# Raw weights of the first expert block in one tile per product, their differences and the gate's steps in another order

## The chip, the core and the metric

The kernel runs on one core of a Trainium2 chip. It is measured in device microseconds (us) from the first to the last instruction. Five engines have queues of their own: TensorE (PE, matrix products), VectorE (DVE), ScalarE (ACT), GpSimd (POOL) and SyncE (SP, which here only issues DMAs). Each runs its list in order and waits on semaphores of the others.

## What is computed

Attention with two masks, then a small mixture of three weight matrices, then a second mixture of eight experts whose gate is normalised by rows and columns eight times. The change lies in the last part:

```python
def _moe2_ref(x, w_gate, w1, w2):          # x: 2304 x 512, w1: 8 x 512 x 1024, w2: 8 x 1024 x 512
    logits = x @ w_gate
    P = np.exp(logits - logits.max())
    for _ in range(8):
        P /= P.sum(1, keepdims=True) + 1e-09
        P /= P.sum(0, keepdims=True) + 1e-09
        P *= N / E
    out = np.zeros((N, D), dtype=np.float32)
    for e in range(E):
        h = np.maximum(x @ w1[e], 0.0)
        out += P[:, e:e + 1] * (h @ w2[e])
    return out
```

## The kernel before

Products keep 32-bit accuracy: every operand is split into a high part (a rounding copy on ACT, L68) and the rest (a subtraction, L69, on POOL for weights), and each product is three passes over such parts (high x high, high x rest, rest x high).

Tokens go in three blocks of 768. The change is in the first of them, where the weights of the experts are prepared as well and kept in DRAM for the two other blocks. This block has 32 stages (L788), one for each of 8 experts `e` and 4 pairs `n` of 128 hidden columns. A stage computes a quarter of x @ w1[e] by a scheme of Strassen's kind, in 7 products of 6 matmuls each (`product`, L803) instead of 8. It needs the weights as they are (`A1` for A11 and A12, `A2` for A22) and differences of them (`S12`, `S34`), made by `sums_w2` (tile `sums`, L538) on DVE and split by `split_w2` (tile `wa`). The products accumulate in two PSUM banks, `p` and `q`, which swap roles from stage to stage, and DVE and ACT turn them into `h`: DVE adds a kept copy (`plus`, L859, tiles `m` and `u`), ACT applies the relu (L853), DVE takes the rest (L854). Between the products PE runs the second product of the stage before (`second`, which calls `Before.tile`, L757), six pieces of 6 matmuls. In the first stage of an expert the finished sums of the expert before are added to the output by an `acc` operation of DVE behind each of the six pieces (L776).

The order of PE in a stage is A11, A12, piece, S2, piece, S1, piece, S3, piece, S4, piece, A22, piece. A12 overwrites the bank that A22 of the stage before filled, so it waits for the two reads of `halves(1, 0, p)`.

Other work runs beside that:

- The raw weights of a stage come in two `raw` tiles, each with rows of w1 and of w2 side by side (`fetch_w2`). The pool has four such tiles.
- The second product's weights are split into `wb` (`split_out`), and their differences are made for the later blocks: `sums_out` (tile `ts`, L577, four operations on DVE) and `keep_out` (split into `tw`, and stored from there).
- In stages 1 to 5 the gate's normalisation runs in steps (`sinkhorn`), some eight small DVE operations at a time (L722 to L739, with L735 reading PSUM), with a small matmul on PE (L734) between, in the bank that `free[0]` names.
- In stages 16, 17, 30 and 31 differences of x for a later block are made (`sums_x`, L602, tiles `xd` and `xh`).

PE, ACT and DVE keep the order in which the code is written. POOL and SP are put in order by a scheduler, with the due times that it reckons. A stage of the code before asks for the next stage's `sums` behind S2, for two gate steps ahead of S2, and ends with `ts` and the next loads:

```python
        second(1, 0)
        more_w("A1")
        window()                       # two steps of the gate
        product(p, "S2", "T2", False, False)
        nc.scalar.copy(u2, p)
        if nxt:
            s_next[0] = sums_w2(nxt)
```

Of the kernel before, what the change touches and what calls it, by code (L numbers as in the profile page):

```python
# [9 lines left out]
F32 = mybir.dt.float32  # L10
# [34 lines left out]
E, F2 = 8, 1024  # L45
P = 128
# [15 lines left out]
NPAIR = NF2 // 2  # L62
# [23 lines left out]
def attention_moe(ctx: ExitStack, tc: tile.TileContext, q, k, v, mask, wm1, wg, wm2, out):  # L86
    nc = tc.nc
# [13 lines left out]
    raw_p = ctx.enter_context(tc.tile_pool(name="raw", bufs=4))  # L101
# [371 lines left out]
    qk, vs, raws = {}, {}, {}  # L473
# [48 lines left out]
    stages = [(0, e, n) for e in range(E) for n in range(NPAIR)]  # L522
    UP = ("A1", "S12", "S34", "A2")

    def fetch_w2(e, n):
        raws = [raw_p.tile([P, 2, 512], F32, name="raw") for _ in range(2)]
        for i in range(2):
            nc.sync.dma_start(raws[i], wm2[e, 2 * n + i])
        return raws

    def sums_w2(raws):
        s = sm_p.tile([P, 4, 256], F32, name="sums")
        (a11, a12), (a21, a22) = ((r[:, 0, 0:256], r[:, 0, 256:512]) for r in raws)
# [10 lines left out]
        for i, name in enumerate(HOLD[what]):  # L544
            ops[name] = t[:, :, i * 256:(i + 1) * 256].rearrange("p s (k m) -> p s k m", k=2)

    def split_w2(i, what, raws, s):

        src = {
            "S12": lambda: s[:, 0:2].rearrange("p o n -> p (o n)"),  # L550
            "S34": lambda: s[:, 2:4].rearrange("p o n -> p (o n)"),
            "A1": lambda: raws[0][:, 0],
            "A2": lambda: raws[1][:, 0, 256:512],
        }[what]()
# [9 lines left out]
        nc.sync.dma_start(t[:, :, 0:w].bitcast(F32), wsd[i % len(stages), UP.index(what), :, :, 0:w])  # L564
        named(w_ops.setdefault(i, {}), what, t)

    def split_out(raws, i):
        t = wb2_p.tile([P, 2, 512], F32R, name="wb2")
        split(nc, t[:, 0], t[:, 1], raws[i][:, 1], nc.gpsimd)
        return t  # L570

    def sums_out(raws):

        s = wt_p.tile([P, 4, 256], F32, name="ts", bufs=1)
        (b11, b12), (b21, b22) = ((r[:, 1, 0:256], r[:, 1, 256:512]) for r in raws)
# [46 lines left out]
    def early():  # L622

        for i in range(2):
            ahead_w[i] = fetch_w2(0, i)
        *_, src = sums_x(fetch_x(0, nc.scalar))
        for i in range(2):
            s = sums_w2(ahead_w[i])
            for what in ("A1", "S12", "S34", "A2"):
                split_w2(i, what, ahead_w[i], s)  # L630
# [5 lines left out]
    ahead_w = {}  # L636

    ahead, starts, gates_due, unit = {}, [], {}, 0
    for what in WORK:
# [147 lines left out]

    for i, (blk, e, n) in enumerate(stages):  # L788
        wo, xo = w_ops.pop(i), x_ops[blk]
        raws = ahead_w.pop(i)  # L790
        nxt = ahead_w.get(i + 1) if i else None
        if i + 2 < len(stages):
            ahead_w[i + 2] = None
        near, last = (e == E - 1 and n == NPAIR - k for k in (2, 1))
        far, farther = (e == E // 2 and n == k for k in (0, 1))
        if near or far:
# [16 lines left out]
                k = NSUB * j + t  # L813
                nc.scalar.mul(acc[k], acc[k], prob[:, k, 0:1])

        def window():
            if i:
                next(gate, None)
                next(gate, None)

        def more_w(what):
            if nxt:
                split_w2(i + 1, what, nxt, s_next[0])
            if i == len(stages) - 1:
# [46 lines left out]
        plus(q, m1)  # L871
        halves(0, 0, m1)
        if i:
            keep_out(i - 1, ts)
        more_x("B21")
        sum_x(last or farther)
        second(1, 0)
        more_w("A1")
        window()
        product(p, "S2", "T2", False, False)  # L880
        nc.scalar.copy(u2, p)
        if nxt:
# [19 lines left out]
        halves(1, 1, m5)  # L902
        sum_x(near or far)
        second(0, 0)
        ws = [split_out(raws, 0)]
        if i == 0:
            gates_turn(B - 1)
            ps_a.release()
# [3 lines left out]
        plus(q, u2)  # L912
        halves(0, 1, u2)
        more_x("B22")
        sum_x(near or far)
        second(0, 1)
        more_w("A2")
        next(gate, None)
        product(p, "A22", "T4", False, True)
        halves(1, 0, p)  # L920
        if i:
            next(gate, None)
        ws.append(split_out(raws, 1))
# [12 lines left out]
    for j in (1, 0):
# [16 lines left out]
    def fetch_out(e, n):  # L953
        t = raw_p.tile([P, 2, 512], F32, name="raw")
        for f in range(2):
            nc.sync.dma_start(t[:, f], wm2[e, 2 * n + f, :, 1])
        return t
# [80 lines left out]

    acc.clear()
    NS = len(stages)  # L1040
    outs = {0: [fetch_out(0, n) for n in range(NPAIR)]}
    for g in range((NBLK - 1) * E):
        blk, e = 1 + g // E, g % E
        sec = Second(blk, e, outs.pop(g))
# [79 lines left out]
        for u in range(len(units)):  # L1124
            sec.product(u)
            if u % NPAIR == NPAIR - 1:
                sec.ready(u // NPAIR)
            if u < 2:
                sec.rows(2 * NPAIR - 2 + u)
                sec.mix(2 + u)  # L1130
            if 2 * NPAIR <= u + 6 < len(units):
                sec.rows(u + 6)
            if 3 * NPAIR <= u + 10 < len(units):
                sec.weight(u + 10)
            if u == 18 and g + 1 < (NBLK - 1) * E:
# [72 lines left out]
```

## Time and profile before

| what | us |
|---|---|
| median of 3 runs | 1917.85 |
| lowest and highest run | 1915.32, 1920.61 |
| span of the profiled execution | 1916.7 |
| PE busy in it | 1864.0 (97%) |
| DVE busy | 1234.4 (64%) |
| ACT busy | 969.2 (51%) |
| POOL busy | 712.5 (37%) |

The profile is of one execution, whose time is its span. The first expert block lies between 428 and 940 us; what stands ahead of it is attention and the first mixture, what follows are the two other blocks. Busy shares are means over parts with different limits, so the block has to be read by itself: which waits PE has in it, and who ends them. A row of the timeline gives the start and the duration of an operation (or of a run of equal ones, with their number), and in brackets how long the engine sat idle before it and who ended that.

### The profile page before, as it was taken

The page shows a single profiled execution, that of the slowest core. Times are in us where ns is not written, and L with a number is a line of the kernel's source. Part 1 is how long each engine was busy: PE and PEld are TensorE (multiplying, and loading weights), DVE is VectorE, ACT ScalarE, POOL GpSimd, SP SyncE. Part 2 cuts the span into 40 slices and gives each one's busy share as a digit, 9 for nine tenths or more (in the row PEclk, how much of TensorE's full clock was granted, in tenths as well). Part 3 has the DMA queues.
Part 4 walks back from the last instruction along what each step waited for, and adds up shares of the span by engine and source line. Part 5 has one row for each costly group of instructions (what it writes and reads, how often), then busy time and mean ns, then how long its engine had stood idle before and what let it go on. Part 6 is the DMA issues. An engine that isn't in the chain of part 4 may idle for free.

```text
span 1916.7 us, 35287 instructions
## 1 busy us (share of the span) xinstructions
PE 1864.0 (97%) x12873; PEld 1793.7 (94%) x12873; DVE 1234.4 (64%) x2227; ACT 969.2 (51%) x2337; POOL 712.5 (37%) x603
## 2 busy tenths in 40 slices
PE   6889999999999999999999999999999999999999
PEld 5789999998899988899899999999999999999999
DVE  7984333426766676666676667766676666766667
ACT  5663544324454444444455555555546555565554
POOL 5663433435566667666611112111112121121211
PEclk8999999999999999999999999999999999999999
DMA  8644444446666669666986767767798767777673
GB/s 266 229 172 160 156 149 160 142 154 217 230 250 250 248 247 330 254 253 248 342 291 216 231 219 221 257 215 226 228 346 254 227 217 224 221 254 227 214 226 111
DMA packets 206542, 435.32 MB, mean 227 GB/s; under 512 B 18848, under 2 KB 97312, under 8 KB 204832
## 3 DMA queue, kind: packets, MB, share of 16 engines
q1 hardware_dynamic: 203680, 429.12, 66.3%
q10 hardware_dynamic: 2688, 3.93, 0.7%
q8 instruction: 102, 1.67, 0.3%
q14 instruction: 72, 0.59, 0.1%
HBM read 313.97 MB, written 119.01 MB: 226 GB/s over the span
## 4 chain that ended last, share of the span: by engine, by line
PE 83%; DVE 7%; DMA 5%; ACT 2%; issue 2%; POOL 1%; SPq 0%; ACTq 0%; DVEq 0%; POOLq 0%
PE po L1006 24%; PE po L1074 12%; PE po L757 10%; PE ps L380 10%; PE q L1074 6%; PE p L1074 6%; PE p L803 5%; PE q L803 5%; PE ps L400 3%; DMA cx<-in_wm 1%; DMA raw<-in_wm 1%; DVE ts L577 1%; DVE h L854 1%; DMA x2s<-xg 1%; PE pst L226 1%
## 5 line engine op out<-in xcount | busy, mean ns | idle before, releaser
L1006 PE MATMUL po<-wt,hop 128*128 128x256 f32 x4032 | 490.3, 284 | 2.1 <-DMA wt<-wtd 2.1
L1006 PEld LDWEIGHTS po<-wt,hop 128*128 128x128 f32 x4032 | 487.8, 192 | 4.1 <-ACT wt L68 2.3
L69 POOL TENSOR_TENSOR wt<-raw,wt 128x256 fp32r<-128x256 f32 x192 | 170.3, 908 | 780.0 <-ACT wt L68 767.8
L69 DVE TENSOR_TENSOR hop<-r,hop 128x384 fp32r<-128x384 f32 x384 | 224.4, 611 | 226.8 <-ACT hop L68 223.2
L757 PE MATMUL po<-wb,h 128*128 128x512 f32 x1152 | 295.6, 393 | 0.9 <-POOL wb L69 0.9
L380 PE MATMUL ps<-xt,wa 128*128 128x288 f32 x1728 | 244.0, 300 | 5.3 <-DVE h L69 3.1
L757 PEld LDWEIGHTS po<-wb,h 128*128 128x128 f32 x1152 | 214.3, 188 | 34.9 <-POOL wb L69 1.7
L380 PEld LDWEIGHTS ps<-xt,wa 128*128 128x128 f32 x1728 | 234.6, 191 | 8.4 <-DVE h L69 3.5
L68 ACT CAST hop<-r 128x384 fp32r<-128x384 f32 x384 | 188.0, 514 | 96.3 <-DVE r L991 74.0
L69 POOL TENSOR_TENSOR wa<-raw,wa 128x512 fp32r<-128x512 f32 x112 | 135.5, 1214 | 76.5 <-ACT wa L68 76.0
L1088 ACT ACTIVATE r<-r 128x384 f32<-128x384 f32 x192 | 99.9, 525 | 117.3 <-DVE r L1087 117.3
L1074 PE MATMUL po<-xT,wa 128*128 128x384 f32 x768 | 155.9, 338 | 0.0
L1074 PEld LDWEIGHTS po<-xT,wa 128*128 128x128 f32 x768 | 136.7, 188 | 0.0
L69 POOL TENSOR_TENSOR tw<-ts,tw 128x512 fp32r<-128x512 f32 x64 | 83.8, 1332 | 95.3 <-DVE h L854 70.6
L1074 PE MATMUL po<-xB,wa 128*128 128x384 f32 x576 | 116.9, 338 | 0.0
L69 POOL TENSOR_TENSOR wa<-sums,wa 128x512 fp32r<-128x512 f32 x64 | 87.3, 1384 | 57.5 <-ACT wa L68 36.8
L1074 PEld LDWEIGHTS po<-xB,wa 128*128 128x128 f32 x576 | 102.5, 188 | 0.0
L69 POOL TENSOR_TENSOR wb<-raw,wb 128x512 fp32r<-128x512 f32 x64 | 93.6, 1462 | 23.5 <-ACT wb L68 22.9
L980 DVE TENSOR_TENSOR r<-r,r 128x384 f32<-128x384 f32 x128 | 93.1, 727 | 2.2
L68 ACT CAST wa<-raw 128x512 fp32r<-128x512 f32 x112 | 61.6, 555 | 59.5 <-DMA raw<-in_wm 32.4
L538 DVE TENSOR_TENSOR sums<-raw 128x256 f32<-128x256 f32 x64 | 41.5, 650 | 74.1 <-DMA raw<-in_wm 73.9
L1019 ACT COPY mm<-po 128x256 f32<-128x256 f32 x144 | 47.0, 376 | 71.0 <-PE po L1006 71.0
(185 smaller groups left out, 3135.7 us busy)
## 6 DMA issues: line engine op xcount, KB each, us to landing
wa<-wsd SPq DMA_DIRECT2D x192, 512.0 KB, 4.4
wt<-wtd SPq DMA_DIRECT2D x256, 256.0 KB, 3.5
wsd<-wa SPq DMA_DIRECT2D x96, 512.0 KB, 3.4
raw<-in_wm SPq DMA_DIRECT2D x64, 512.0 KB, 4.3
wtd<-tw SPq DMA_DIRECT2D x128, 256.0 KB, 2.9
raw<-in_wm SPq DMA_DIRECT2D x128, 256.0 KB, 5.2
wa<-wsd SPq DMA_DIRECT2D x64, 256.0 KB, 4.5
cx<-in_wm SPq DMA_DIRECT2D x12, 1024.0 KB, 6.8
```

Of the source, the lines that this page charges most:

```text
L68: nc.scalar.copy(hi, src)
L69: sub.tensor_tensor(out=lo, in0=src, in1=hi.bitcast(F32), op=ALU.subtract)
L380: nc.tensor.matmul(ps, w[:, wi, kk], xt[:, xi, kk, n0:n0 + HB], start=(n == 0), stop=(n == 3 * KT - 1),)
L400: nc.tensor.matmul(ps, wo[f][:, wi, d2 * P:(d2 + 1) * P], hs[f][:, hi, a * HB:(a + 1) * HB], start=(f == 0 and n == 0), stop=(f == NF1 - 1 ...
L538: nc.vector.tensor_tensor(out=s[:, o], in0=x, in1=y, op=op)
L757: nc.tensor.matmul(po, self.hs[f, j][:, hi, t * P:(t + 1) * P], self.ws[f][:, wi], start=(n + f + k == 0), stop=(n == NPAIR - 1 and f == 1 ...
L803: nc.tensor.matmul(ps, wo[w][:, wi, kk], xo[x][:, xi, kk], start=(first and k == 0), stop=True if k == 5 else False, skip_group_check=not ...
L980: nc.vector.tensor_tensor(out=r[o, n], in0=r[x, n], in1=r[y, n], op=op)
L1006: nc.tensor.matmul(self.ps[side, t][:, 0:256], h[:, hi, t * P:(t + 1) * P], w[:, wi], start=(first and i == 0), stop=(n == NPAIR - 1 and i ...
L1019: nc.scalar.copy(m, ps)
L1074: nc.tensor.matmul(ps[k][side], wo[k][w][:, wi, kk], xo[x][:, xi, kk], start=(first and c == 0), stop=c == 5, skip_group_check=not first,)
L1088: nc.scalar.activation(out=r, in_=r, func=AF.Relu)
```

## The change

- A `raw` tile no longer holds rows of w1 and w2 side by side. `fetch_w2` takes a third argument and loads, by two DMAs of 256 KB, either the w1 part of both row groups (`ups`) or the w2 part (`downs`). `fetch_out` of the later blocks, which did this already, is gone in its favour.
- A stage's w1 tile is loaded behind the last use of the tile two stages ahead of it (`fetch_up(i + 3)` behind the split of `A2`), its w2 tile in the stage before (`fetch_down(i + 1)`).
- `sums_out` moves from the end of a stage into the next stage, behind `plus` and the first `halves`.
- The two gate steps that stood ahead of S2 come one behind S2 and one behind `sums`.
- The second step of `sum_x` of stages 16 and 30 moves from behind `halves(0, 1)` to behind `halves(1, 0)`.

```diff
-    def fetch_w2(e, n):
-        raws = [raw_p.tile([P, 2, 512], F32, name="raw") for _ in range(2)]
-        for i in range(2):
-            nc.sync.dma_start(raws[i], wm2[e, 2 * n + i])
-        return raws
+    def fetch_w2(e, n, part):
+        t = raw_p.tile([P, 2, 512], F32, name="raw")
+        for f in range(2):
+            nc.sync.dma_start(t[:, f], wm2[e, 2 * n + f, :, part])
+        return t
+
+    def fetch_up(i):
+        if i < len(stages):
+            ups[i] = fetch_w2(*stages[i][1:], 0)
+
+    def fetch_down(i):
+        if i < len(stages):
+            downs[i] = fetch_w2(*stages[i][1:], 1)
...
         for i in range(2):
-            ahead_w[i] = fetch_w2(0, i)
+            fetch_up(i)
+        for i in range(2):
+            fetch_down(i)
...
-        def window():
+        def step():
             if i:
                 next(gate, None)
-                next(gate, None)
...
         halves(0, 0, m1)
         if i:
-            keep_out(i - 1, ts)
+            keep_out(i - 1, sums_out(downs.pop(i - 1)))
+            fetch_down(i + 1)
         more_x("B21")
         sum_x(last or farther)
         second(1, 0)
         more_w("A1")
-        window()
         product(p, "S2", "T2", False, False)
         nc.scalar.copy(u2, p)
-        if nxt:
+        step()
+        if nxt is not None:
             s_next[0] = sums_w2(nxt)
+        step()
...
         more_x("B22")
-        sum_x(near or far)
         second(0, 1)
         more_w("A2")
+        if i:
+            fetch_up(i + 3)
         next(gate, None)
         product(p, "A22", "T4", False, True)
         halves(1, 0, p)
-        if i:
-            next(gate, None)
-        ws.append(split_out(raws, 1))
-        ts = sums_out(raws)
+        sum_x(near or far)
+        step()
+        ws.append(split_out(down_raw, 1))
         more_x("T3")
         keep_x(3)
         keep_x(4)
         second(0, 2)
         more_x("T4")
-        if i + 2 < len(stages):
-            ahead_w[i + 2] = fetch_w2(*stages[i + 2][1:])
```

The lists of ACT and POOL are the same before and after. DVE's list, from the last gate operation of stage 2 into stage 3 (`m` is `plus`, `h` the rest of a relu, `sms` a sum of the gate that reads PSUM in L735), before:

```order
L729 TENSOR_REDUCE sms<-prob 128x8
L577 TENSOR_TENSOR ts<-raw 128x256
L577 TENSOR_TENSOR ts<-raw,ts 128x256
L577 TENSOR_TENSOR ts<-raw 128x256
L577 TENSOR_TENSOR ts<-raw,ts 128x256
L859 TENSOR_TENSOR m_5519<-p,m_5519 128x384
L854 SCALAR_TENSOR_TENSOR h_5513<-m_5519,h_5513 128x384
L735 TENSOR_SCALAR sms<-p 128x8
L737 RECIPROCAL sms<-sms 128x8
L738 TENSOR_SCALAR sms<-sms 128x8
```

The same place after (the line numbers have moved by 8 to 12):

```order
L741 TENSOR_REDUCE sms<-prob 128x8
L868 TENSOR_TENSOR m_5524<-p,m_5524 128x384
L863 SCALAR_TENSOR_TENSOR h_5518<-m_5524,h_5518 128x384
L585 TENSOR_TENSOR ts<-raw 128x256
L585 TENSOR_TENSOR ts<-raw,ts 128x256
L585 TENSOR_TENSOR ts<-raw 128x256
L585 TENSOR_TENSOR ts<-raw,ts 128x256
L747 TENSOR_SCALAR sms<-p 128x8
L546 TENSOR_TENSOR sums<-raw 128x256
L546 TENSOR_TENSOR sums<-sums,raw 128x256
L546 TENSOR_TENSOR sums<-raw 128x256
L546 TENSOR_TENSOR sums<-raw,sums 128x256
```

The four `ts` have moved behind `m` and `h`, and the four `sums` of the next stage, which came behind eight operations of the gate, follow L735 at once.

PE's list in stage 3, from A11 to the piece behind S2, before:

```order
L803 MATMUL q<-xB_4297,wa 128x384 x6
L803 MATMUL p<-xB_4329,wa 128x384 x6
L757 MATMUL po_5212<-wb_5454,h_5344 128x512 x3
L757 MATMUL po_5212<-wb_5495,h_5346 128x512 x3
L734 MATMUL p<-sms,ones 128x8
L803 MATMUL q<-xT_4822,wa 128x384 x6
L757 MATMUL po_5238<-wb_5454,h_5344 128x512 x3
```

And after:

```order
L813 MATMUL q<-xB_4297,wa 128x384 x6
L813 MATMUL p<-xB_4329,wa 128x384 x6
L769 MATMUL po_5221<-wb_5465,h_5347 128x512 x3
L769 MATMUL po_5221<-wb_5509,h_5349 128x512 x3
L813 MATMUL q<-xT_4832,wa 128x384 x6
L746 MATMUL p<-sms,ones 128x8
L769 MATMUL po_5247<-wb_5465,h_5347 128x512 x3
```

The small matmul of the gate, which writes the bank that `m` reads, stands behind S2 instead of ahead of it. The second one of a stage, ahead of A22, keeps its place.

SP's list of two stages (`wtd` takes the `tw` tiles, `wsd` the `wa` tiles), before:

```order
L528 DMA raw<-in_wm 128x1024 x2
L585 DMA wtd<-tw 256x1x256 x4
L558 DMA wsd<-wa 128x1024 x3
L558 DMA wsd<-wa 256x1x256
L528 DMA raw<-in_wm 128x1024 x2
```

And after:

```order
L528 DMA raw<-in_wm 128x512 x4
L593 DMA wtd<-tw 256x1x256 x4
L566 DMA wsd<-wa 128x1024 x3
L566 DMA wsd<-wa 256x1x256
L528 DMA raw<-in_wm 128x512 x4
```

The four loads are two of a w1 tile, asked for at the end of a stage, and two of a w2 tile, asked for behind `ts` of the next.

## Rows read from the trace of the kernel before

**Rows 1.** The waits from 430 to 960 us: who for whom, total, times, longest.

```profile
DVE sums L538 <- DMA raw<-in_wm: 73.7, 26, 4.1
...
PE p L803 <- DVE h L854: 4.7, 4, 2.4
...
PE p L734 <- DVE m L859: 3.2, 2, 1.6
```

**Rows 2.** Stretches: length, then busy time of each engine, PE clock, DMA share, GB/s.

```profile
527.00:690.00 163.00, 163.00 (x817) 147.58 (x816) 104.74 (x172) 82.49 (x162) 106.27 (x85) 1.00 0.69 251
496.00:498.00 2.00, 2.00 (x8) 1.59 (x7) 1.92 (x3) 1.26 (x3) 2.00 (x2) 0.64 1.03 424
498.00:500.00 2.00, 2.00 (x7) 1.88 (x6) 1.90 (x4) 1.14 (x3) 1.73 (x2) 0.51 0.95 328
```

**Rows 3.** Timeline of PE in stage 3: start, duration, operation.

```profile
471.70 1.21 PE L803 MATMUL q<-xB,wa 128*128 128x384 f32 x6
...
476.94 0.39 PE L734 MATMUL p<-sms,ones 128*128 128x8 f32 x2 [1.60 <-DVE m L859]
...
486.98 0.28 PE L734 MATMUL p<-sms,ones 128*128 128x8 f32 x2
...
489.63 1.21 PE L803 MATMUL p<-xB,wa 128*128 128x384 f32 x6
```

**Rows 4.** Timeline of DVE in stage 3.

```profile
474.88 0.41 DVE L577 TENSOR_TENSOR ts<-raw 128x256 f32<-128x256 f32 x1
...
476.34 0.55 DVE L859 TENSOR_TENSOR m<-p,m 128x384 f32<-128x384 f32 x1
...
477.95 0.16 DVE L735 TENSOR_SCALAR sms<-p 128x8 f32<-128x8 f32 x1
...
478.39 0.97 DVE L738 TENSOR_SCALAR sms<-sms 128x8 f32<-128x8 f32 x1
...
482.96 0.41 DVE L538 TENSOR_TENSOR sums<-raw 128x256 f32<-128x256 f32 x1
...
484.43 0.55 DVE L859 TENSOR_TENSOR m<-q,m 128x384 f32<-128x384 f32 x1
...
486.20 0.54 DVE L859 TENSOR_TENSOR u<-p,u 128x384 f32<-128x384 f32 x1
```

**Rows 5.** Timeline of ACT and POOL in stage 3.

```profile
477.35 1.13 ACT L68 CAST tw<-ts 128x512 fp32r<-128x512 f32 x2
...
478.03 1.30 POOL L69 TENSOR_TENSOR tw<-ts,tw 128x512 fp32r<-128x512 f32 x1 [4.89 <-ACT tw L68]
```

**Rows 6.** Timeline of DVE and POOL at 751 us, end of stage 19.

```profile
751.28 0.83 DVE L577 TENSOR_TENSOR ts<-raw 128x256 f32<-128x256 f32 x1
...
752.67 1.46 POOL L69 TENSOR_TENSOR wb<-raw,wb 128x512 fp32r<-128x512 f32 x1
...
752.92 1.50 DVE L577 TENSOR_TENSOR ts<-raw 128x256 f32<-128x256 f32 x1
...
754.34 1.23 DVE L577 TENSOR_TENSOR ts<-raw,ts 128x256 f32<-128x256 f32 x1
```

**Rows 7.** Timeline of DVE and PE in stage 8 and at its end.

```profile
560.61 0.56 DVE L859 TENSOR_TENSOR m<-q,m 128x384 f32<-128x384 f32 x1
...
567.11 0.42 DVE L538 TENSOR_TENSOR sums<-raw,sums 128x256 f32<-128x256 f32 x1
...
573.42 0.55 DVE L854 SCALAR_TENSOR_TENSOR h<-p,h 128x384 fp32r<-128x384 f32 x1
...
574.90 1.22 PE L803 MATMUL p<-xB,wa 128*128 128x384 f32 x6
```

**Rows 8.** Timeline of DVE and PE at the ends of stages 16 and 20.

```profile
699.66 1.49 DVE L602 TENSOR_TENSOR xh<-xh 128x768 f32<-128x768 f32 x1
...
702.34 1.32 PE L803 MATMUL p<-xB,wa 128*128 128x384 f32 x6 [2.36 <-DVE h L854]
...
769.36 1.32 PE L803 MATMUL p<-xB,wa 128*128 128x384 f32 x6 [0.94 <-DVE h L854]
```

More of the change, by code (lines that the diff above doesn't have):

```diff
@@ L523, in attention_moe, with sums_w2 @@
     UP = ("A1", "S12", "S34", "A2")
-    def fetch_w2(e, n):
-        raws = [raw_p.tile([P, 2, 512], F32, name="raw") for _ in range(2)]
-        for i in range(2):
-            nc.sync.dma_start(raws[i], wm2[e, 2 * n + i])
-        return raws
-    def sums_w2(raws):
+    def fetch_w2(e, n, part):
[9 more added lines that the diff above has]
+            downs[i] = fetch_w2(*stages[i][1:], 1)
+    def sums_w2(raw):
         s = sm_p.tile([P, 4, 256], F32, name="sums")
-        (a11, a12), (a21, a22) = ((r[:, 0, 0:256], r[:, 0, 256:512]) for r in raws)
+        (a11, a12), (a21, a22) = ((raw[:, f, 0:256], raw[:, f, 256:512]) for f in range(2))
         for o, x, y, op in (
@@ L545, in named, with split_w2 @@
             ops[name] = t[:, :, i * 256:(i + 1) * 256].rearrange("p s (k m) -> p s k m", k=2)
-    def split_w2(i, what, raws, s):
+    def split_w2(i, what, raw, s):
         src = {
@@ L551, in split_w2 @@
             "S34": lambda: s[:, 2:4].rearrange("p o n -> p (o n)"),
-            "A1": lambda: raws[0][:, 0],
-            "A2": lambda: raws[1][:, 0, 256:512],
+            "A1": lambda: raw[:, 0],
+            "A2": lambda: raw[:, 1, 256:512],
         }[what]()
@@ L565, in load_w2, with split_out, sums_out @@
         named(w_ops.setdefault(i, {}), what, t)
-    def split_out(raws, i):
+    def split_out(raw, f):
         t = wb2_p.tile([P, 2, 512], F32R, name="wb2")
-        split(nc, t[:, 0], t[:, 1], raws[i][:, 1], nc.gpsimd)
+        split(nc, t[:, 0], t[:, 1], raw[:, f], nc.gpsimd)
         return t
-    def sums_out(raws):
+    def sums_out(raw):
         s = wt_p.tile([P, 4, 256], F32, name="ts", bufs=1)
-        (b11, b12), (b21, b22) = ((r[:, 1, 0:256], r[:, 1, 256:512]) for r in raws)
+        (b11, b12), (b21, b22) = ((raw[:, f, 0:256], raw[:, f, 256:512]) for f in range(2))
         for o, x, y in ((0, b12, b11), (1, b22, s[:, 0]), (2, b22, b12), (3, b21, s[:, 1])):
@@ L624, in early @@
         for i in range(2):
-            ahead_w[i] = fetch_w2(0, i)
+            fetch_up(i)
+        for i in range(2):
+            fetch_down(i)
         *_, src = sums_x(fetch_x(0, nc.scalar))
         for i in range(2):
-            s = sums_w2(ahead_w[i])
+            raw = ups.pop(i)
+            s = sums_w2(raw)
             for what in ("A1", "S12", "S34", "A2"):
-                split_w2(i, what, ahead_w[i], s)
+                split_w2(i, what, raw, s)
+            fetch_up(i + 2)
         for i, name in enumerate(("T2", "T1", "T3", "T4")):
@@ L635, in attention_moe @@
     x_ops = {i: {} for i in range(NBLK + 1)}
-    ahead_w = {}
+    ups, downs = {}, {}
     ahead, starts, gates_due, unit = {}, [], {}, 0
@@ L789, in attention_moe @@
         wo, xo = w_ops.pop(i), x_ops[blk]
-        raws = ahead_w.pop(i)
-        nxt = ahead_w.get(i + 1) if i else None
-        if i + 2 < len(stages):
-            ahead_w[i + 2] = None
+        down_raw = downs[i]
+        nxt = ups.pop(i + 1, None) if i else None
         near, last = (e == E - 1 and n == NPAIR - k for k in (2, 1))
@@ L878, in attention_moe @@
         more_w("A1")
-        window()
         product(p, "S2", "T2", False, False)
         nc.scalar.copy(u2, p)
-        if nxt:
+        step()
+        if nxt is not None:
             s_next[0] = sums_w2(nxt)
+        step()
         more_x("T2")
@@ L904, in attention_moe @@
         second(0, 0)
-        ws = [split_out(raws, 0)]
+        ws = [split_out(down_raw, 0)]
         if i == 0:
@@ L929, in attention_moe @@
         more_x("T4")
-        if i + 2 < len(stages):
-            ahead_w[i + 2] = fetch_w2(*stages[i + 2][1:])
         before = Before((blk, e, n), hs, ws, po, acc)
-    keep_out(len(stages) - 1, ts)
+    keep_out(len(stages) - 1, sums_out(downs.pop(len(stages) - 1)))
     for what in UP:
@@ L951, in attention_moe @@
     units = [(k, n) for k in range(7) for n in range(NPAIR)]
[L953 to L957, printed above, removed]
     class Second:
@@ L1040, in attention_moe @@
     NS = len(stages)
-    outs = {0: [fetch_out(0, n) for n in range(NPAIR)]}
+    outs = {0: [fetch_w2(0, n, 1) for n in range(NPAIR)]}
     for g in range((NBLK - 1) * E):
@@ L1135, in attention_moe @@
             if u == 18 and g + 1 < (NBLK - 1) * E:
-                outs[g + 1] = [fetch_out((e + 1) % E, n) for n in range(NPAIR)]
+                outs[g + 1] = [fetch_w2((e + 1) % E, n, 1) for n in range(NPAIR)]
     fixed.close()
```

## Prediction

> **What bounds the kernel now.** I looked first for waits of TensorE (PE) inside the first expert block, since only PE's order decides its end. In the waits of that stretch [rows 1] the largest name in the change's way is VectorE (DVE): 73.7 us in 26 waits for a raw weight tile, in front of `sums`. That looks like a prize, but the view of stretches denies it: from 527 to 690 us PE is busy 163.00 of 163.00 us [rows 2], ten stages in a row in which DVE waits for raw tiles all the same. Idle time of an engine that is not late costs nothing. What PE loses in the block are a few short waits: for `h` (4.7 us, 4 times) and, in the gate's steps, for DVE's `m` (3.2 us in the two for bank `p`) [rows 1]. Besides, PE's granted clock fell to 0.64 and 0.51 between 496 and 500 us [rows 2], behind two of these waits; at 2 x 0.36 + 2 x 0.49 that cost 1.7 us.
>
> So I read one stage with gate steps (stage 3) on PE and on DVE. PE takes 17.93 us from one A11 to the next (471.70 to 489.63) and waits 1.60 us at the first small matmul of the gate (L734) at 476.94; the second, at 486.98, starts with no wait [rows 3]. DVE has no gap there that the order could fill: `ts` at 474.88, `m` at 476.34, the gate's L735 at 477.95, its eight small operations until `sums` at 482.96, `m` again at 484.43, `u` at 486.20, done at 486.74 [rows 4]. That is only 0.24 us ahead of PE's second small matmul, which writes the bank that `u` reads. The loop therefore closes over DVE: A22, relu, `h`, all of DVE's list, `u`, small matmul, A22. A wait taken off the first small matmul alone comes back at the second, but for 0.24 us.
>
> **The part that decides: who is beside DVE.** In order, POOL does `tw` twice, then A1, S12, S34, `wb`, A2, `wb`, before and after. In stage 3 it starts `tw` at 478.03, 0.68 us behind the start of ACT's cast at 477.35 [rows 5]. Beside it the eight-element L738 took 0.97 us on DVE where the equally small L735 took 0.16 [rows 4]: a blocked operation loses some 0.8 us. What happens when POOL has one operation behind the other stands at 751 us, after the same list: the four `ts` of DVE begin at 751.28 and the last at 754.34; 752.92 took 1.50 us instead of 0.42, because POOL's `wb` at 752.67 ran until 754.13, and the next began 1.42 us after it [rows 6]. So DVE gets one such operation in per operation of POOL, at about 1.4 us each. An operation that reads PSUM (`m` at 476.34 and 484.43) keeps its 0.55 us [rows 4].
>
> The change puts `ts` behind `m` and `h`, and `sums`, whose input is there by then, right behind `ts` (in gate stages behind L735): into the stretch in which POOL runs `tw`, `tw`, A1 and then S12 without a gap. Before, `sums` had to wait for its tile or for the gate, and POOL had by then run dry: 482.96 to 484.43 is 1.47 us for the four [rows 4].
>
> **Stages 2 to 5, worked out on stage 3.** After: `m` at 474.88 (in the place of `ts`), `h` 1.14 us later as before (relu between), `ts` at 476.49 with 0.34 us each, L735 at 477.85, first `sums` at 478.05. ACT can cast `tw` when the second `ts` has landed, at 477.25; plus the 0.68 us of [rows 5] POOL starts at 477.93 and has the port by 0.12 us. Four `sums` at 1.4 us end at 483.65. The eight gate operations took 4.81 us before (478.15 to 482.96), three of them blocked; I leave one blocked (by S12 or S34): 4.81 - 2 x 0.8 = 3.2. `m` comes at 486.85 instead of 484.43, 2.4 us later, and so does `u`. PE, freed of its first wait, stands at the second small matmul for longer. The stage grows by 2.4 - 0.24 = 2.2 us. Low end: the first `sums` wins the port (0.34 + 3 x 1.4 = 4.5) and no gate operation is blocked (2.4): `m` at 485.0, +0.3 us. High end: two gate operations still blocked (4.0) and each `sums` costs 1.6: 488.5, +3.8. I take 2.2, because the run of four at 751 us is the nearest row. Four stages: **+8.8** (1.2 to 15). Stage 1 has only the first steps of the gate: +0.5 (0 to 1).
>
> The Trainium skill ("SBUF — State Buffer", section Who interferes with whom) speaks against the change here: a DVE instruction with two SBUF inputs and a POOL instruction that reads SBUF exclude each other for the whole instruction, whoever issues first. By it each `sums` would wait out a whole `tw` or A1 and then run, 1.27 + 0.34 = 1.6 us, an estimate that makes stages 2 to 5 worth 4 x 0.8 = 3.2 us more; the 1.42 us of 752.92 to 754.34 [rows 6] is less than that, so the trace has the two overlap a little, and the sum keeps 1.4.
>
> **Stages with accumulation.** In the first stage of an expert DVE also has six `acc` operations. There the last `sums` starts at 567.11 and `h` of A22 at 573.42, which ends at 573.97; A12 of the next stage, which overwrites that bank, starts at 574.90 [rows 7]: 0.93 us to spare. After: `m` at 560.61, `h` 1.14 later, `ts` from 562.23, first `acc` until 564.25; POOL has `tw` from 563.67 (second `ts` landed at 562.99, plus 0.68), so `sums` start behind it at 564.9 and then every 1.4, the last at 569.1: 2.0 us later than now, 1.1 more than there is to spare. If one of the four is not blocked, 0.6 later: nothing. I take 0.7, nearer the upper end. Stage 20 waits already (0.94 us [rows 8]); stages 8, 12, 16, 24 and 28: **+3.5** (0 to 6).
>
> **What goes.** In stage 17 PE waits 2.36 us because `h` of A22 stands behind an `xh` of 1.49 us and `acc` [rows 8]; the change moves that subtraction behind `h`: **-2.4** (0 to -3; the subtraction is then late for stage 17's `m`). In plain stages (neither gate nor `acc`) nothing changes for PE: `sums` ending some 6 us after A12 is still ahead of `m`, which needs S3. The four 256 KB loads in place of two of 512 KB cost SP two more issues per stage, and on SP's queue four stores of `tw` stand behind them; these are needed a stage later, so I price that at nothing (0 to +0.5). The front of the block orders the loads differently and waits for nothing new. The second phase keeps its code. Clock: the dip of 1.7 us may go with the short waits or come again with longer ones; I take no change (-1.7 to +5).
>
> **Sum.** 8.8 + 0.5 + 3.5 - 2.4 = +10.4 us on the profiled execution of 1916.7, so 1927.1; the median of the runs, 1917.85, stands 1.15 above it: **1928 us**, 0.5% slower.
>
> **Rivals.**
> Faster: `sums` gets through before POOL begins. It needs `tw` on POOL 1.4 us later than 477.93, or DVE winning every time. Then the chain keeps its length, gate stages give 4 x 0.24, `acc` stages nothing, stage 17 gives 2.4, stage 20 gives 0.94 and the dip of 1.7 goes: 1917.85 - 6.0 = 1912. For it: the two times lie 0.12 us apart. Against it: POOL is back for the next operation within 0.1 us, so a first win leaves three to be blocked.
> No change: the low ends hold. 4 x 0.3 in gate stages, nothing in `acc` stages, -2.4 in stage 17: 1917, between 1913 and 1923. For it: at 567.11 and around, `sums` lost only one operation to POOL. The loads not coming a stage early would end here too, since DVE would wait as now.
> Clock: PE's waits at the second small matmul would be over 3 us in each of four stages, and the clock falls behind waits as at 496 us. Three more dips of 1.7: 1933. Against it: the 2.36 us of stage 17 did no harm.
>
> **How the numbers follow.** Forecast (1922 to 1931) 0.55, clock 0.12, no change 0.20, faster 0.13. Range for 8 in 10: 1912 to 1936, which leaves out the lower half of the faster case and little above. A change under 0.3% (1912.1 to 1923.6) can't be told from none here: slower 0.66, same 0.21, faster 0.13.
>
> **What would show it.** Right: PE's wait at the first small matmul gone, one of 2.5 to 4 us at the second in stages 2 to 5; the four `sums` spaced by 1.4 us beside `tw`, `tw`, A1; DVE's 73.7 us for raw tiles gone, with no gain; a new wait of about 1 us at A12 behind `acc` stages. Wrong: `sums` spaced by 0.34 us, or POOL's `tw` starting after them; then the sum falls to the faster case.

## The result and the profile after the change

The changed kernel took 1936.94 us (median of 4 runs, 1934.22 to 1937.33) against 1918.63 for the kernel before on the same chip (4 runs): a ratio of 1.010, 95% interval 1.0083 to 1.0117. It is slower, as forecast, but by 18.3 us instead of 10, and 0.9 us above the upper end of the range. The same kernel measured again beside the last experiments gave 1933.72 us, ratio 1.0085 (1.0072 to 1.0097), inside the range.

To see where the time went I use one measure throughout: the length of the first expert block from the start of A11 in stage 0 to the start of A11 in stage 31, and its stages from A11 to A11. Two profiles of the changed kernel give 512.12 and 512.28 us, although their spans are 1935.4 and 1929.3: what differs between these two runs of one kernel lies ahead of the block and behind it. The block of the kernel before is 495.92 us. So the change cost 16.2 us in the block; what it did outside, if anything, is lost in that scatter.

| stages | before, us | after, us | difference |
|---|---|---|---|
| 0 and 1 | 25.93 | 25.91 | 0.0 |
| 2, 3, 4, 5 (gate) | 17.15, 17.93, 19.47, 17.91 | 19.37, 22.43, 21.21, 20.95 | +11.5 |
| 8 and 9, likewise 12, 24, 28 with the next | 31.22 | 32.61 | +1.38 each, +5.5 |
| 16 and 17 | 33.86 | 34.66 | +0.8 |
| 18 and 19 | 33.31 | 31.26 | -2.1 |
| 20 and 21 | 33.71 | 34.19 | +0.5 |
| all others | 15.61 each | 15.61 each | 0.0 |

The waits of the changed kernel from 430 to 960 us (who for whom, total, times, longest) show the two main places:

```profile
PE p L746 <- DVE u L868: 6.4, 2, 3.4
PE p L813 <- DVE h L863: 6.4, 8, 1.0
PE q L746 <- DVE u L868: 6.1, 2, 3.0
```

PE now waits four times, 3.0 to 3.4 us each, for `u` at the second small matmul of the gate (L746), and eight times up to 1.0 us for `h` at A12 (four times before). The wait for `m` at the first small matmul [rows 1] is gone, and so is DVE's wait for raw tiles, all 73.7 us of it. It paid mainly in stages 18 and 19 (as it does in e1 below, which has the new loads alone). There, in the kernel before, `sums` waited 3.79 and 3.92 us for their tiles and then stood beside POOL's reads, and PE was held up in stage 19 (0.51 us for `h`, 0.36 us for `m`):

```profile
725.29 0.87 DVE L538 TENSOR_TENSOR sums<-raw 128x256 f32<-128x256 f32 x1 [3.79 <-DMA raw<-in_wm]
...
734.75 1.32 PE L803 MATMUL p<-xB,wa 128*128 128x384 f32 x6 [0.51 <-DVE h L854]
```

The two stages took 15.97 and 17.34 us before and 15.61 and 15.65 after.

**A gate stage.** Stage 3 on DVE, the counterpart of [rows 4] (start, duration, operation):

```profile
481.29 0.16 DVE L747 TENSOR_SCALAR sms<-p 128x8 f32<-128x8 f32 x1
481.37 0.41 DVE L546 TENSOR_TENSOR sums<-raw 128x256 f32<-128x256 f32 x1
481.81 1.41 DVE L546 TENSOR_TENSOR sums<-sums,raw 128x256 f32<-128x256 f32 x1
483.14 1.52 DVE L546 TENSOR_TENSOR sums<-raw 128x256 f32<-128x256 f32 x1
484.58 1.50 DVE L546 TENSOR_TENSOR sums<-raw,sums 128x256 f32<-128x256 f32 x1
486.01 0.19 DVE L749 RECIPROCAL sms<-sms 128x8 f32<-128x8 f32 x1
486.24 1.04 DVE L750 TENSOR_SCALAR sms<-sms 128x8 f32<-128x8 f32 x1
487.31 1.36 DVE L751 TENSOR_TENSOR prob<-prob,sms 128x144 f32<-128x144 f32 x1
...
490.22 0.55 DVE L868 TENSOR_TENSOR m<-q,m 128x384 f32<-128x384 f32 x1
...
491.83 0.55 DVE L868 TENSOR_TENSOR u<-p,u 128x384 f32<-128x384 f32 x1
```

And on POOL:

```profile
481.48 2.90 POOL L69 TENSOR_TENSOR tw<-ts,tw 128x512 fp32r<-128x512 f32 x2 [5.21 <-ACT tw L68]
484.34 1.47 POOL L69 TENSOR_TENSOR wa<-raw,wa 128x512 fp32r<-128x512 f32 x1
485.77 2.73 POOL L69 TENSOR_TENSOR wa<-sums,wa 128x512 fp32r<-128x512 f32 x2
```

The first `sums` slips in 0.11 us ahead of POOL's `tw` and takes 0.41 us. The next three start 1.33 to 1.44 us apart, about as POOL's operations do (1.45 for each `tw`). L750 and L751 of the gate are held up too, by `S12` and `S34`. From L747 to `m` it is 8.93 us, and `u` is late by it. PE in the same stage:

```profile
475.07 1.21 PE L813 MATMUL q<-xB,wa 128*128 128x384 f32 x6
...
487.52 1.54 PE L769 MATMUL po<-wb,h 128*128 128x512 f32 x6
492.43 0.59 PE L746 MATMUL p<-sms,ones 128*128 128x8 f32 x2 [3.38 <-DVE u L868]
492.88 2.27 PE L813 MATMUL q<-xT,wa 128*128 128x384 f32 x6
494.94 2.76 PE L769 MATMUL po<-wb,h 128*128 128x512 f32 x6
497.50 1.48 PE L813 MATMUL p<-xB,wa 128*128 128x384 f32 x6
```

The last rows show a second loss: behind the wait, six matmuls take 2.27 us instead of 1.21 and a piece 2.76 instead of 1.54. The view of stretches has PE's granted clock (after the busy times) at the lower of its two levels there:

```profile
492.00:494.00 2.00, 1.57 (x6) 1.57 (x7) 1.07 (x3) 0.82 (x2) 1.86 (x2) 0.50 0.16 59
494.00:496.00 2.00, 2.00 (x7) 1.81 (x6) 0.29 (x1) 0.82 (x2) 0.18 (x1) 0.50 0.30 102
496.00:498.00 2.00, 2.00 (x6) 1.61 (x6) 1.90 (x5) 0.18 (x1) 1.28 (x1) 0.50 0.99 260
```

It falls again in stages 4 and 5, not in stage 2.

**A stage with accumulation.** Stage 8 on DVE, the counterpart of [rows 7]:

```profile
573.26 0.56 DVE L868 TENSOR_TENSOR m<-q,m 128x384 f32<-128x384 f32 x1 [2.04 <-PE q L813]
...
577.02 1.11 DVE L546 TENSOR_TENSOR sums<-raw 128x256 f32<-128x256 f32 x1
578.16 1.40 DVE L546 TENSOR_TENSOR sums<-sums,raw 128x256 f32<-128x256 f32 x1
579.48 1.51 DVE L546 TENSOR_TENSOR sums<-raw 128x256 f32<-128x256 f32 x1
580.92 1.52 DVE L546 TENSOR_TENSOR sums<-raw,sums 128x256 f32<-128x256 f32 x1
...
588.23 0.55 DVE L863 SCALAR_TENSOR_TENSOR h<-p,h 128x384 fp32r<-128x384 f32 x1
```

The last `sums` ends 9.18 us behind the start of `m` (582.44 less 573.26); before, it was 6.92 (567.53 less 560.61). DVE is 2.26 us later, which is more than the 0.93 us that A12 had to spare, and PE waits for `h` at the A12 that follows:

```profile
588.83 1.32 PE L813 MATMUL p<-xB,wa 128*128 128x384 f32 x6 [0.80 <-DVE h L863]
```

### The profile page after: what moved, and what is told of

It is laid out like the page before. It is cut to its first block, busy times and chain, and to the rows that moved or that the text cites. A ratio compares the mean times of both kernels' runs of the same rounds, so it can differ in the third digit from the quotient of the medians.

```text
span 1935.4 us, 35368 instructions
## 1 busy us (share of the span) xinstructions
PE 1875.9 (97%) x12873; PEld 1803.1 (93%) x12873; DVE 1285.1 (66%) x2227; ACT 970.2 (50%) x2337; POOL 721.5 (37%) x603
## 4 chain that ended last, share of the span: by engine, by line
PE 79%; DVE 10%; DMA 4%; issue 2%; ACT 2%; POOL 1%; SPq 0%; DVEq 0%; ACTq 0%; POOLq 0%
PE po L1009 24%; PE po L1077 12%; PE ps L380 10%; PE po L769 8%; PE q L1077 6%; PE p L1077 6%; PE p L813 4%; PE q L813 4%; PE ps L400 3%; DVE sums L546 3%; DMA cx<-in_wm 1%; DVE acc L788 1%; DMA x2s<-xg 1%; ACT h L862 1%; DVE h L863 1%
## 5 line engine op out<-in xcount | busy, mean ns | idle before, releaser
L69 POOL TENSOR_TENSOR tw<-ts,tw 128x512 fp32r<-128x512 f32 x64 | 91.8, 1455 | 129.8 <-ACT tw L68 125.5
L69 POOL TENSOR_TENSOR wb<-raw,wb 128x512 fp32r<-128x512 f32 x64 | 89.4, 1397 | 38.4 <-ACT wb L68 37.8
L813 PE MATMUL q<-xT,wa 128*128 128x384 f32 x384 | 80.0, 344 | 0.9 <-DVE m L868 0.9
L863 DVE SCALAR_TENSOR_TENSOR h<-m,h 128x384 fp32r<-128x384 f32 x64 | 54.8, 856 | 39.0 <-ACT h L862 39.0
```

Of the source, the lines that this page charges most:

```text
L813: nc.tensor.matmul(ps, wo[w][:, wi, kk], xo[x][:, xi, kk], start=(first and k == 0), stop=True if k == 5 else False, skip_group_check=not ...
L863: nc.vector.scalar_tensor_tensor(out=h[:, 1], in0=c, scalar=0.0, in1=h[:, 0].bitcast(F32), op0=ALU.max, op1=ALU.subtract)
```

## The experiments

The theory was that POOL's reads hold up DVE's `sums` and gate operations because `sums` now stand beside POOL's run of `tw`, `tw`, A1; that the new loads cost nothing; and that the clock adds to it behind PE's longer waits. The rivals: the loads or the move of `ts` cost the time, or the clock is most of it. The table gives the median, the ratio to the kernel before (95%), the block from A11 of stage 0 to A11 of stage 31, and stages 2 to 5.

| run | median, us | ratio to before | block, us | stages 2 to 5, us |
|---|---|---|---|---|
| before | 1918.63 | 1 | 495.92 | 17.15, 17.93, 19.47, 17.91 |
| after | 1936.94 | 1.0083 to 1.0117 | 512.12 | 19.37, 22.43, 21.21, 20.95 |
| e1_loads_alone | 1912.89 | 0.9968 to 0.9993 | 492.53 | 16.80, 17.89, 17.87, 17.90 |
| e2_gate_back | 1922.36 | 1.001 to 1.0035 | 499.52 | 17.18, 17.95, 17.95, 17.96 |
| e3_sums_late | 1914.04 | 0.9974 to 0.9993 | 491.80 | 17.17, 17.94, 17.96, 17.96 |
| e4_warm | 1929.3 | 1.0041 to 1.0071 | 508.01 | 19.43, 20.11, 20.16, 20.16 |
| e5_tw_no_read | 1908.4 | 0.9927 to 0.9969 | 486.15 | 16.86, 17.60, 17.22, 17.58 |
| e6_ts_end | 1926.77 | 1.0029 to 1.0057 | 502.86 | 19.02, 22.43, 18.50, 22.44 |
| e7_loads_gates | 1912.97 | 0.9963 to 0.9991 | 489.98 | 16.81, 17.63, 16.09, 17.74 |
| e8_late_gates | 1911.62 | 0.9957 to 0.9983 | 488.94 | 17.19, 16.27, 17.18, 16.28 |
| f1_after | 1933.72 | 1.0072 to 1.0097 | 512.28 | 19.36, 22.43, 21.37, 20.97 |
| f2_warm | 1928.56 | 1.004 to 1.0064 | 507.98 | 19.42, 20.13, 20.15, 20.18 |
| f3_acc_late | 1926.75 | 1.0035 to 1.0059 | 506.28 | 20.82, 21.04, 20.96, 21.92 |
| f4_sumx_back | 1936.74 | 1.0089 to 1.0115 | 513.80 | 19.36, 22.44, 21.20, 20.92 |

The kernel before took 1917.76 us beside e1 to e4, 1917.03 beside e5 to e8 and 1917.81 beside f1 to f4.

### The loads alone

The new tiles and loads with DVE's and the gate's order of before (against the changed kernel):

```diff
-            keep_out(i - 1, sums_out(downs.pop(i - 1)))
+            keep_out(i - 1, ts)
...
+        step()
+        step()
         product(p, "S2", "T2", False, False)
...
+        ts = sums_out(downs.pop(i))
+        fetch_down(i + 2)
```

> The order of before on every engine, with the changed kernel's tiles and early loads alone. Theory (DVE's sums stand beside POOL's tw and A1 and are blocked; the loads do no harm): at or below the kernel before, 1913 to 1918 us, since the late sums of stages 18 to 20 go; gate stages as before, 17.2 to 17.9 us each with one wait of about 1.6 us at the first small matmul. Rival (the loads themselves cost: twice as many, of 2 KB rows, in bursts ahead of the stores of tw): most of the 18 us are there, 1928 to 1937 us.

It took 1912.89 us, 4.9 below the kernel before. So the loads are no cost; they are a small gain, which the order more than uses up. By the block the gain is 3.4 us: the clock's fall of 1.6 us in stage 4 is not there, and stages 18 to 21 together are 2.4 us shorter; against that, stage 17 is 1.0 longer, because the clock fell there behind a wait of 1.81 us. Only the 2.4 us can be traced to the loads: the wait at the first small matmul of stage 4 is 1.53 us in both profiles, and the clock fell behind it in one.

### Which move costs it

Both gate steps back ahead of S2, all else as changed:

```diff
+        step()
+        step()
         product(p, "S2", "T2", False, False)
         nc.scalar.copy(u2, p)
-        step()
         if nxt is not None:
             s_next[0] = sums_w2(nxt)
-        step()
```

> The changed kernel with the two gate steps ahead of S2 as before, so that sums come behind eight operations of the gate again, when POOL has done tw and A1. Theory: gate stages go back to 17 to 18 us, the waits of over 3 us at the second small matmul shrink below 1.5 us, and with them the falls of PE's clock go; the waits behind acc operations (about 1.4 us for each of six experts) stay: 1937 - 11.5 = 1925 us, 1923 to 1928. Rival (the ts operations behind m and h are what costs): 1933 us or more.

`sums` behind the piece that follows S1, the gate's steps as changed:

```diff
-        if nxt is not None:
-            s_next[0] = sums_w2(nxt)
...
         second(1, 2)
+        if nxt is not None:
+            s_next[0] = sums_w2(nxt)
         more_w("S12")
```

> The changed kernel with sums moved down, behind the piece after S1, so that they run when POOL has done tw and A1; the rest of the change stays. Theory: both places heal, gate stages 17 to 18 us and no wait behind acc operations: 1914 to 1920 us. Rival (what costs is not the place of sums beside POOL, but the gate steps behind S2 or the loads): above 1928 us.

`ts` back at the stage's end, the gate and `sums` as changed:

```diff
-            keep_out(i - 1, sums_out(downs.pop(i - 1)))
+            keep_out(i - 1, ts)
...
         ws.append(split_out(down_raw, 1))
+        ts = sums_out(downs.pop(i))
+        fetch_down(i + 2)
```

> The changed kernel with the four ts operations at the end of the stage as before; the early loads, the later gate steps and sums behind S2 stay. Theory: the waits behind acc operations (1.4 us for an expert) go, since sums end 1.4 us earlier, but gate stages still take about 20 us with sums beside tw and A1, and the clock still falls: 1930 us (1927 to 1933). Rival (ts behind m and h is the cause in the gate stages too): 1920 us or less.

In e2 and in e3 the gate stages are back at 17.2 and 17.95, with no fall of the clock, because in both the eight gate operations again stand between L747 and `sums`. Stage 3 of e3 on POOL and on DVE:

```profile
476.26 2.54 POOL L69 TENSOR_TENSOR tw<-ts,tw 128x512 fp32r<-128x512 f32 x2 [5.01 <-ACT tw L68]
478.76 1.35 POOL L69 TENSOR_TENSOR wa<-raw,wa 128x512 fp32r<-128x512 f32 x1
```

```profile
476.07 0.16 DVE L747 TENSOR_SCALAR sms<-p 128x8 f32<-128x8 f32 x1
...
476.50 1.07 DVE L750 TENSOR_SCALAR sms<-sms 128x8 f32<-128x8 f32 x1
477.61 1.35 DVE L751 TENSOR_TENSOR prob<-prob,sms 128x144 f32<-128x144 f32 x1
...
479.33 0.81 DVE L735 TENSOR_SCALAR sk<-sk 128x18 f32<-128x18 f32 x1
...
481.17 0.41 DVE L546 TENSOR_TENSOR sums<-raw 128x256 f32<-128x256 f32 x1
...
482.29 0.42 DVE L546 TENSOR_TENSOR sums<-raw,sums 128x256 f32<-128x256 f32 x1
482.63 0.55 DVE L868 TENSOR_TENSOR m<-q,m 128x384 f32<-128x384 f32 x1
```

POOL has run dry at 480.11, and the four `sums` take some 1.5 us instead of 4.64. Three of the gate's eight operations are now held up beside `tw` and A1 (L750, L751, L735), where in the changed kernel it was two, but from L747 to `m` it is 6.56 us instead of 8.93. The stages with accumulation part the two: e2 keeps their +1.38, since without gate operations `sums` follow `ts` there as in the changed kernel; in e3 they are 15.61 and 15.70. In e6 it is the other way round. Its gate stages stay long (waits of 2.7, 3.0, 1.8 and 3.0 us at the second small matmul) and the stages with accumulation are 15.61. So the gate's loss hangs on where `sums` stand, the other on `sums` and `ts` in the same stretch. e2 came out at 1922.4, just under its range, e6 at 1926.8, 0.2 under, e3 in its range.

### POOL without reads

POOL fills `tw` with zeros instead of subtracting.

```diff
-            split(nc, t[:, 0], t[:, 1], s[:, o:o + 2].rearrange("p o n -> p (o n)"), nc.gpsimd)
+            nc.scalar.copy(t[:, 0], s[:, o:o + 2].rearrange("p o n -> p (o n)"))
+            nc.gpsimd.memset(t.bitcast(F32), 0.0)
```

> The changed kernel in the same order, but POOL fills tw with zeros (about 1.06 us for 1024 columns, by the 0.53 us that 512 took) instead of subtracting (1.27 us): it is busy nearly as long, but reads no SBUF. The differences for the later blocks are left out by that, so the work of those blocks is on zeros. Theory (DVE's sums are blocked by POOL's reads): the four sums run at 0.34 us beside the two fills, gate stages take 17.5 to 18.2 us, no wait behind acc operations: 1912 to 1919 us. Rival (POOL's being busy, or the semaphores between DVE, ACT and POOL, slow the sums): spaced by over 1 us as before, above 1930 us.

The order is that of the changed kernel, yet it took 1908.4 us, below its range and 25 to 29 us below the two medians of the changed kernel. Stage 3 on DVE and on POOL:

```profile
479.64 0.42 DVE L546 TENSOR_TENSOR sums<-raw 128x256 f32<-128x256 f32 x1
480.10 0.43 DVE L546 TENSOR_TENSOR sums<-sums,raw 128x256 f32<-128x256 f32 x1
480.44 0.42 DVE L546 TENSOR_TENSOR sums<-raw 128x256 f32<-128x256 f32 x1
480.77 0.42 DVE L546 TENSOR_TENSOR sums<-raw,sums 128x256 f32<-128x256 f32 x1
...
481.64 1.37 DVE L752 TENSOR_TENSOR prob<-prob,sms 128x144 f32<-128x144 f32 x1
```

```profile
479.74 1.85 POOL L592 MEMSET tw<- 128x1024 f32 x2 [5.19 <-ACT tw L591]
481.55 1.30 POOL L69 TENSOR_TENSOR wa<-raw,wa 128x512 fp32r<-128x512 f32 x1
```

The last three `sums` lie wholly inside POOL's two fills, the first all but its first 0.10 us, and all four keep 0.42 us. As soon as POOL reads again (A1 at 481.55), a gate operation with two inputs in SBUF takes 1.37 us; in the changed kernel it takes 0.31 us at 476.33, where POOL stands idle. This settles the cause: not that POOL is busy, but that it reads. The Trainium skill ("SBUF — State Buffer", section Who interferes with whom) says the same, that a DVE instruction with two SBUF inputs contends with a GpSimd instruction that reads SBUF and not with one that only writes it; these rows agree.

### The clock by itself

Twelve matmuls with zero weights ahead of the second small matmul in stages 2 to 5; they add zero to a sum that is open anyway.

```diff
+        if 2 <= i <= 5:
+            for _ in range(12):
+                nc.tensor.matmul(
+                    po[2 if before.stage[2] else 0], zeros, before.ws[0][:, 0],
+                    start=False, stop=False, skip_group_check=True,
+                )
         next(gate, None)
         product(p, "A22", "T4", False, True)
```

> The changed kernel with twelve matmuls with a zero weight (2.6 us of work, they add zero to an open sum) in front of the second small matmul of stages 2 to 5, where PE waits 3.0 to 3.4 us. If the falls of the clock come from these waits: no fall to 0.5 behind them, 5.8 us less, 1931 us (1929 to 1933). If they come from something else: 1937 us or more. The waits of DVE's chain themselves stay, so it can't come near the kernel before.

PE in stage 3:

```profile
484.03 2.96 PE L934 MATMUL po<-wb,zeros 128*128 128x512 f32 x12
487.58 0.39 PE L748 MATMUL p<-sms,ones 128*128 128x8 f32 x2 [0.59 <-DVE u L870]
487.82 1.30 PE L815 MATMUL q<-xT,wa 128*128 128x384 f32 x6
488.96 1.53 PE L771 MATMUL po<-wb,h 128*128 128x512 f32 x6
```

The small matmul comes no earlier, but the work behind it runs at 1.30 and 1.53 us instead of 2.27 and 2.76. The medians of two sets of runs differed by 7.6 us, the stages of the two profiles by 4.1 (83.96 less 79.86), so both kernels ran once more side by side:

> The changed kernel itself once more, as the base for the three beside it. 1936.5 us (1934 to 1938).

> The changed kernel with twelve zero-weight matmuls ahead of the second small matmul of the gate in stages 2 to 5, again, beside the changed kernel itself. Theory: the falls of the clock cost what the four stages show in the profiles, 4.1 us, so it lies 3 to 5 us below the changed kernel (1932). Rival: the falls cost the 7.6 us by which the two medians differed, also behind the four stages; then 6.5 to 8.5 below (1929).

f1 came out 0.3 us under its range. The medians now lie 5.2 us apart, just above what the theory gave, and the blocks 4.3 (that f2's own time is close to the rival's 1929 us comes from f1's being lower than expected). So the falls cost about 4 to 5 us; of the first 7.6 the rest lies outside the block (4.1 us within it).

### The stages with accumulation and the moved subtraction

`sums` late only in the first stage of an expert:

```diff
-        if nxt is not None:
+        if nxt is not None and i not in (8, 12, 16, 20, 24, 28):
             s_next[0] = sums_w2(nxt)
...
+        if nxt is not None and i in (8, 12, 16, 20, 24, 28):
+            s_next[0] = sums_w2(nxt)
         more_w("S12")
```

> The changed kernel, but in the stages with accumulation (8, 12, 16, 20, 24, 28) the sums stand behind the piece after S1. Theory: sums blocked by POOL are the whole of the lateness there, so the four plain ones give back 1.38 us each and stages 16 to 21 some 0.5: 5 to 7 us below the changed kernel (1930.5). Rival, by the prediction's term of 0.7 for each of five: 3.5 below (1933). Rival that the acc operations are late for another reason: 0 to 1 below.

It took 1926.75 us, 7.0 below the changed kernel, at the upper end of the theory and twice what the prediction's term gives. The stages are 15.61 and 15.70 again, and stages 16 to 21 give 2.0 us where 0.5 was expected. The block is 6.0 shorter although the clock cost about 1 us more here: it fell in all four gate stages.

`sum_x` back ahead of the piece:

```diff
         more_x("B22")
+        sum_x(near or far)
         second(0, 1)
...
         halves(1, 0, p)
-        sum_x(near or far)
```

> The changed kernel with the one subtraction of x in stages 16 and 30 back ahead of the piece, where the kernel before has it. Theory: the subtraction of 1.5 us stands in front of the h for which PE waits 0.96 us at the end of stage 16, so the wait grows by about 1.5 and the move is still worth that: 1 to 2 us above the changed kernel (1938). Rival by the prediction's term: 2.4 us above. Rival that the late sums have eaten the whole gain: no difference.

It took 1936.74 us. That is 3.0 above the changed kernel, but the runs of the two overlap (1936.21 to 1940.34 and 1931.13 to 1937.25), so the block has to decide: it is 1.5 longer, within the theory, and the place is stage 17 (19.90 against 18.13). The rows of PE tell how that comes about, those of f4 first:

```profile
716.77 1.32 PE L813 MATMUL p<-xB,wa 128*128 128x384 f32 x6 [2.36 <-DVE h L863]
717.92 2.70 PE L769 MATMUL po<-wb,h 128*128 128x512 f32 x6
```

and of the changed kernel:

```profile
717.35 1.32 PE L813 MATMUL p<-xB,wa 128*128 128x384 f32 x6 [0.96 <-DVE h L863]
...
730.68 1.32 PE L813 MATMUL q<-xT,wa 128*128 128x384 f32 x6 [0.92 <-DVE m L868]
```

With the subtraction moved, the wait of 2.36 us at A12 becomes one of 0.96 there and one of 0.92 at S4, whose `m` stands behind the late operations. In waits the move is worth 0.5 us; the rest is the clock, which fell in f4 behind 2.36 us: the view of stretches has it at 0.50 from 718 to 720 us, and a piece takes 2.70 us instead of 1.54:

```profile
718.00:720.00 2.00, 2.00 (x7) 1.51 (x6) 1.22 (x3) 0.52 (x1) 0.00 (x0) 0.50 0.25 95
```

### A better order

What is left in the gate stages of e1 and e3 is DVE's list itself. Two variants spread the gate over more stages, with two steps fewer in stages 3 and 5 and those steps in stage 6 instead: e7 on the base of e1 (but with the later `sum_x` of the changed kernel), e8 on that of e3.

```diff
+    HEAVY = (1, 2, 4, 6)
...
-        next(gate, None)
+        if not i or i in HEAVY:
+            next(gate, None)
         product(p, "A22", "T4", False, True)
...
-        step()
+        if i in HEAVY:
+            step()
```

> The order of before with the early loads (as e1), with the later second step of sum_x, and with the gate's iterations spread over stages 1 to 6: two in stages 2, 4 and 6, one in stages 3 and 5. Theory: the gate's cost is DVE's chain in a stage with two iterations, 17.9 us against 15.6; one iteration fits into a stage. So one heavy stage less and stage 17 without its wait: 2 to 4 us below e1, 1909 to 1911 us. Rival (a gate step costs the same wherever it is put): as e1, 1913 us.

> e3 (the changed kernel with sums behind the piece after S1) with the same spreading of the gate. Theory: one heavy stage less than e3, 1911 to 1913 us. Rival as for e7: 1914 us.

e8 took 1911.62 us, ratio 0.997 (0.9957 to 0.9983): faster than both kernels, in its range. Stages 3 and 5 fall to 16.3 us, and the block is 488.94, 7.0 us below the kernel before. So a stage with one iteration still takes some 0.7 us more than a plain one of 15.61. e7 missed: its stages 4 and 6 fall to 16.1 and its block is 2.6 us shorter than that of e1, but its median is the same (1912.97 against 1912.89), so these runs do not tell the two apart. Of the 2.6 us, 1.7 come from stages 2 to 6 and 1.8 from stage 17, where `sum_x` stands later; stages 20 and 21 take 0.9 back.

## Why the prediction was right in sign and short in size

The sum of the prediction against the block, term by term:

| term | forecast, us | measured, us |
|---|---|---|
| waits in stages 2 to 5 | +8.8 | +9.0 |
| stage 1 | +0.5 | 0.0 |
| stages 8, 12, 24, 28 | +2.8 | +5.5 |
| stages 16 and 17 | -1.7 | +0.8 |
| stages 18 to 21 | 0 | -1.6 |
| clock in stages 2 to 5 | 0 | +2.5 |
| sum | +10.4 | +16.2 |

The gate's row is that of e4, where the clock does not fall, less the stages before without their fall (79.86 less 70.89, with 17.90 taken for stage 4 by its neighbours); the clock's row is 4.1 after less 1.6 before.

- **What bounds the kernel** was right for the stretch that it read, 527 to 690 us. But the sentence that nothing changes for PE in plain stages does not hold behind it: the early loads took 2.1 us off stages 18 and 19 (33.31 to 31.26, and 31.22 in e1, which has the loads alone).
- **Who is beside DVE** was right, and e5 shows it. One `sums` gets in per operation of POOL, 1.40 us each (486.01 less 481.81, by three), as taken from 751 us [rows 6]; the 1.6 us of the whole-instruction estimate was too much. Of the two `m` that it gives for reads of PSUM only the one at 484.43 stands beside POOL (busy from 484.57); it kept its 0.55 us, and so did `u` at 486.20.
- **Stages 2 to 5** came out at 2.2 to 2.3 us each without the clock, as forecast, partly by two errors that cancel. The first `sums` won against POOL (4.64 us for four where 5.6 was taken), which is the low end; but two gate operations were held up instead of one (4.21 us from the last `sums` to `m` where 3.2 was taken), which is the high end.
- **The stages with accumulation** were mis-sized: 0.7 us taken, 1.38 measured. The mechanism held. The sum had worked out 1.1 itself and then took off part for the case that one of the four is not blocked; in fact all four are (1.11 to 1.52 us each in stage 8), and DVE is 2.26 us late against 0.93 to spare. The 0.6 us of that case is too low as well: an operation that is not blocked still takes 0.34, so by the sum's own terms the last `sums` start 0.9 us late, which is all that there is to spare.
- **What goes** failed too, and luck hides part of it. Stage 17 was to lose its wait of 2.36 us and gave 0.1 (18.24 to 18.15). The prediction said in a bracket that the moved subtraction is then late for stage 17's `m`, and its sum took nothing for that: it is the 0.92 us at S4. Besides, PE still waits in stage 17 for `h` at A12, 0.96 us (0.95 in f3, so not for the `sums`), and 0.46 us for `u` at A11 (gone in f3, so for the `sums` of stage 16, whose lateness was forecast). That the stages from 16 to 21 together still came out 0.8 shorter is the unforecast gain of stages 18 and 19.
- **The clock** is the step that failed most plainly. The sum put it at nothing and gave the rival, waits over 3 us in all four stages, 0.12. But its own terms say otherwise: the first wait of 1.6 us goes to the second small matmul, and 2.2 come on top, so some 3.8 us were to be expected there; the prediction itself names a wait of 2.5 to 4 us there as a sign of being right. Measured are 3.0 to 3.4, and the clock fell behind three of the four. The argument against it, that 2.36 us at stage 17 did no harm, does not bear weight either: at the same place the clock fell in f4 behind 2.36 us and in e1 behind 1.81. With the falls taken out the same order took 1929.3 and 1928.56 us (e4, f2) and stood inside the range, with the block 12.1 us longer than before where 10.4 was forecast.
- **The range** took the clock's 5 us in, but not together with the misses of the other stages. All of them add up to 5.8 us in the block; with 2 us more outside it, which is within the scatter there, they passed its end. The second median of the same kernel lies inside the range, so on which side of its end the time came out is chance.

The rival that the loads do not come early fell, as DVE no longer waits for them. The faster case fell with the rows of stage 3: DVE did win the first time, and three operations were still blocked.

Open: why the clock fell in stage 2 only in f3, behind the same wait (3.05 us) as in the other profiles (3.04), and why the times outside the block differ by some us from run to run (A11 of stage 0 starts between 424.9 and 430.6 us).

## What to carry to other kernels

Before you move a DVE operation with two SBUF inputs earlier because its data are there, look what POOL reads at that time: here four operations of 0.4 us cost 4.6 us beside POOL's reads and 1.5 us once POOL had run dry. Where the gate's operations must pass anyway, put them beside POOL's run and the four large ones behind it: between L747 and `m` that left three operations blocked in e3, where the changed kernel has five. And when a sum says that TensorE will wait longer in one place, price the clock behind that wait in the same sum, not as a rival with a small chance.

## What the runs showed of the hardware

- POOL's subtraction `tw` and DVE's differences alternate, one for one: 1.41 to 1.52 us for a DVE operation of 0.42 (stage 3 of the changed kernel), and 1.45 us for each of POOL's, which take 1.27 us where only short operations of the gate stand beside them (2.54 for two in e3).
- A fill on POOL, which reads nothing, left four such DVE operations at 0.42 to 0.43 us. An eight-element operation beside POOL's reads took 1.04 us instead of 0.17. A reduction (0.30 us, L734 at 479.00 in e3) and an addition that reads PSUM (0.54 us, `u` at 486.20 in the kernel before) kept their time there.
- Behind waits of 3.0 to 3.4 us the granted clock fell to 0.50 in three of four stages, in f3 in all four; at stage 17 it fell behind 2.36 us in f4 and behind 1.81 us in e1, but not behind 2.36 us in the kernel before. In the kernel before it fell behind 1.53 us in stage 4, and not behind the same 1.53 us in e1. So a wait's length alone did not decide it here. Twelve matmuls with zero weights in the wait kept it at 1.00 in both profiles.
